# Attention output made by token and transposed by DMA, in batches 4 to 7 of a fused attention and bilinear FFN kernel

## Chip, cores, metric

One core of one Trainium2 chip. The metric is device time in microseconds (us) of one execution; times quoted are medians of several runs. The engines are PE (TensorE matmuls; PEld is its weight loading), VectorE (DVE in the profile), ScalarE (ACT), GpSimd (POOL) and SyncE (SP, which here only issues DMAs). In the timelines below each works through its own instructions in program order; the wait of 12.96 us shown there comes of it. The rounds ran on several chips, and each ratio compares runs of the same rounds. In this text a profile line such as "L255" is line 255 of that kernel; the changed kernel has other numbers for the same code.

## The reference

```python
# q, k, v: (8 batches, 8 heads, 576 tokens, 64), float32
kv  = einsum('bhsd,bhse->bhde', k, v)            # 64x64 per head
o   = einsum('bhsd,bhde->bhse', q, kv)
rms = sqrt(mean(o * o, axis=-1) + 1e-6)          # over the 64 of a head
x   = (o / rms * g_norm)  -> (4608 tokens, 512)
out = ((x @ w_a) * (x @ w_b)) @ w_out            # 512 -> 1536 -> 512
```

## The kernel before

The FFN runs in nine strips of 512 tokens (numbered from 0). A strip is 12 units (4 matmuls with w_a, 4 with w_b; ScalarE copies the first sum, VectorE multiplies the second by it: "ab product"), then 4 output groups of 12 matmuls. The x of batch s+1 is made in the gaps of strip s. It is made with the features on partitions, as the FFN needs it: product, square, a matmul with a block of ones (which sums the squares over a head's 64 partitions and copies the sum to all of them), root, product with g.

```python
    def psq(self, p, i0):                                   # ScalarE
        nc.scalar.activation(sq[p % 3], P[:, i0 : i0 + 2, 0:HF], AF.Square)
    def pss(self, p, i0, hs=(0, 1)):                        # PE, ScalarE
        for h in hs:
            nc.tensor.matmul(P[:, i0 + h, 0:HF], lhsT=ones, rhs=sq[p % 3][:, h, :], ...)
        nc.scalar.activation(rs[p % 3][...], P[...], AF.Abs_reciprocal_sqrt, bias=eps_t)
    def pst(self, p, x0, hs=(0, 1)):                        # VectorE: P * g * rs -> xt[p]
        ...
    def x(self, p, i0):                                     # PE, 288 columns each
        for h in range(2):
            nc.tensor.matmul(P[:, i0 + h, 0:HF], lhsT=kvb[self.b % 2][:, p, :],
                             rhs=self.qT[:, p, h * HF : (h + 1) * HF], ...)

def load_late(b):                                           # all on GpSimd
    if b > EARLY:
        nc.gpsimd.tensor_copy(gate, qT[(b - 1) % 2][0:1, 0, 0:1])   # waits for a q transpose
    ...                       # six DMA issues: q to a DRAM buffer (2), k (2), v (2)

def transpose_q(b):
    nc.sync.dma_start_transpose(qT[b % 2], qs_d[b])

for s in range(1, N_STRIP - 1):
    b = s + 1
    A = Attn(b) if b < B else None
    for n in range(FC + 4):
        amid = (lambda n=n: slot(A, s, n - 0.5)) if A else None
        ...                                   # FFN unit or output group n; amid() inside it
        if A:
            slot(A, s, n)                     # a piece of the work for x of batch b
        if n == 8 and b + 1 < B:
            if s > 1:
                transpose_q(b + 1)
                if b + 2 < B:
                    load_late(b + 2)
            ...
```

The gate is a one-element copy that keeps the late load of batch b+2 from starting before the q of batch b+1 has been transposed. [cuts are marked by "..."]

## Time and profile before

| | before |
|---|---|
| time, median of 4 runs beside the changed kernel | 321.39 us (321.21 to 322.28) |
| span in the profile, granted PE clock | 319.4 us, 1.000 |
| strips 1 to 6, each | 33.9 us |

Lines of the page of the kernel before: busy time by engine, the granted clock in 40 slices (9 is 90% or more), the chain that ended last, and groups of instructions (line, engine, operation, output<-inputs, shapes, count | busy us, mean ns | idle before it and who ended that).

```profile
PE 312.0 (98%) x1848; PEld 150.2 (47%) x1883; DVE 124.6 (39%) x218; ACT 125.3 (39%) x217; POOL 70.2 (22%) x94
...
PEclk9999999999999999999999999999999999999999
...
PE 93%; POOL 3%; DMA 2%; issue 1%; ACT 0%; POOLq 0%
...
L273 DVE TENSOR_TENSOR ab<-P,asb 128x512 bf16<-128x512 f32 x108 | 74.5, 691 | 124.0 <-PE P L255 120.7
...
L126 POOL COPY gate<-qT 1x1 bf16<-1x1 bf16 x5 | 0.9, 176 | 83.2 <-DMA qT<-qs 83.2
L209 PE MATMUL P<-sq,ones 128*128 128x288 bf16 x64 | 13.2, 286 | 0.5 <-ACT sq L205 0.4
L235 PE MATMUL P<-qT,kvb 128*128 128x288 bf16 x56 | 11.4, 286 | 0.0
```

PE is the limit: it is busy nearly all the time and is nearly all of the chain. The mean of 286 ns is the length of one matmul's record; the records overlap, and the timeline shows a pair of these matmuls taking 0.24 us from its first start to the start of what follows, 0.12 us each. VectorE idles 120.7 us waiting for PE (L273), so it has room.

Stretches of the kernel before: start:end, length, then busy us of PE, PEld, DVE, ACT, POOL, granted clock, DMA share, GB/s. These are strips 3 to 5.

```profile
118.33:152.22 33.89, 33.73 (x198) 16.28 (x200) 13.45 (x22) 14.39 (x24) 7.00 (x8) 1.00 1.26 151
152.22:186.12 33.90, 33.69 (x198) 16.29 (x200) 13.45 (x22) 14.39 (x24) 6.57 (x7) 1.00 0.73 102
186.12:220.02 33.90, 33.69 (x198) 16.30 (x200) 13.45 (x22) 14.39 (x24) 0.00 (x0) 1.00 0.17 46
```

Timeline of the kernel before around the late load of strip 4, SyncE's and GpSimd's queues (start, length, engine, line, operation).

```profile
153.39 2.24 SPq L141 DMA_TRANSPOSE qT<-qs  x1
159.02 0.18 POOL L126 COPY gate<-qT 1x1 bf16<-1x1 bf16 x1 [19.17 <-DMA qT<-qs]
159.50 3.26 POOL L129 DMA_DIRECT2D qs<-in_q_dram  x2 [0.30 <-issue]
...
165.18 0.72 POOL L136 DMA_DIRECT2D vtl<-in_v_dram  x1
```

GpSimd stands at the gate for 19.17 us. That costs nothing here, as nothing else is queued on it. Note two lengths: 5.6 us from the issue of the transpose to the gate, and 6.9 us from the gate to the end of the last issue.

### The profile page before, as it was taken

To read this page: it belongs to the slowest core of one execution; us is meant where nothing else is said; L and a number is where in the kernel's file an instruction comes from. 1 tells how busy PE (TensorE), PEld (TensorE's weight loads), DVE (VectorE), ACT (ScalarE), POOL (GpSimd) and SP (SyncE) were. 2 spreads that over 40 slices of the span, in tenths; PEclk is the share of its full clock that TensorE was granted. 3 is DMA by queue.
4 is the path that set the end of the run, shared out by engine and by line. 5 is a ranking of instruction groups with operands and counts; after the bars stand their busy time and mean duration, and the time that the engine had idled before them with its cause. 6 is when DMAs were issued, how large, how long until landed. Compare 5 with 4: busy or idle time off the path is not lost.

```text
span 319.4 us, 4695 instructions
## 1 busy us (share of the span) xinstructions
PE 312.0 (98%) x1848; PEld 150.2 (47%) x1883; DVE 124.6 (39%) x218; ACT 125.3 (39%) x217; POOL 70.2 (22%) x94
## 2 busy tenths in 40 slices
PE   8899999999999999999999999999999999999995
PEld 3444454444445444444444444444544444444443
DVE  5543344444244333452245324532364243313421
ACT  3733165354335443542445225542454323123310
POOL 8944990070043080350070000000000000000000
PEclk9999999999999999999999999999999999999999
DMA  8999999999379999899499150003000200020002
GB/s 182 197 196 199 201 182 230 141 95 161 99 92 159 135 123 211 81 138 173 119 94 129 66 139 2 0 35 100 0 2 14 90 30 0 34 84 18 0 33 99
DMA packets 79308, 32.60 MB, mean 102 GB/s; under 512 B 49974, under 2 KB 74806, under 8 KB 79286
## 3 DMA queue, kind: packets, MB, share of 16 engines
q0 software_dynamic: 59120, 18.44, 53.0%
q1 hardware_dynamic: 19810, 13.44, 17.1%
q10 hardware_dynamic: 356, 0.43, 0.4%
q8 instruction: 14, 0.23, 0.3%
q14 instruction: 8, 0.07, 0.1%
HBM read 37.75 MB, written 12.98 MB: 159 GB/s over the span
## 4 chain that ended last, share of the span: by engine, by line
PE 93%; POOL 3%; DMA 2%; issue 1%; ACT 0%; POOLq 0%
PE P L255 58%; PE P L309 29%; PE P L209 2%; PE P L235 2%; DMA wb_t<-in_moe_w_b_dram 2%; PE P L158 2%; POOL vt L106 1%; POOL qt L106 1%; POOL kt L106 1%; PE P L182 0%; POOL wa_t L367 0%; POOL wb_t L367 0%; ACT o_end L540 0%; POOL ident masks.py:199 0%; POOL ident masks.py:197 0%
## 5 line engine op out<-in xcount | busy, mean ns | idle before, releaser
L273 DVE TENSOR_TENSOR ab<-P,asb 128x512 bf16<-128x512 f32 x108 | 74.5, 691 | 124.0 <-PE P L255 120.7
L255 PE MATMUL P<-xt,wa_t 128*128 128x512 bf16 x422 | 111.2, 379 | 0.9 <-issue 0.2
L255 PE MATMUL P<-xt,wb_t 128*128 128x512 bf16 x421 | 110.1, 379 | 0.3
L309 PE MATMUL P<-wo_t,ab 128*128 128x512 bf16 (+1 forms) x431 | 97.5, 373 | 0.7
L269 ACT CAST asb<-P 128x512 bf16<-128x512 f32 x108 | 63.0, 585 | 85.3 <-PE P L255 83.8
L255 PEld LDWEIGHTS <-wb_t 128*128 128x128 bf16 x432 | 42.3, 98 | 50.6 <-DMA wb_t<-in_moe_w_b_dram 0.5
L309 PEld LDWEIGHTS <-ab 128*128 128x128 bf16 x444 | 43.1, 98 | 45.4
L255 PEld LDWEIGHTS <-wa_t 128*128 128x128 bf16 x432 | 41.7, 98 | 45.1 <-issue 0.5
L223 DVE SCALAR_TENSOR_TENSOR xt<-P,g_col,rs 128x288 bf16<-128x288 f32 x64 | 30.1, 513 | 29.6 <-ACT rs L213 29.6
L205 ACT ACTIVATE sq<-P 128x576 bf16<-128x576 f32 x31 | 20.2, 650 | 25.1 <-PE P L235 23.2
L213 ACT ACTIVATE rs<-P,eps_t 128x576 f32<-128x576 f32 (+1 forms) x33 | 23.9, 727 | 14.9 <-PE P L209 14.6
L322 ACT COPY osb<-P 128x512 f32<-128x512 f32 x17 | 10.0, 586 | 46.0 <-PE P L309 43.6
L324 DVE COPY osb<-P 128x512 f32<-128x512 f32 x18 | 12.4, 691 | 26.9 <-PE P L309 26.8
L129 POOL DMA_DIRECT2D qs<-in_q_dram x12 | 19.6, 1636 | 2.2 <-issue 2.1
L126 POOL COPY gate<-qT 1x1 bf16<-1x1 bf16 x5 | 0.9, 176 | 83.2 <-DMA qT<-qs 83.2
L209 PE MATMUL P<-sq,ones 128*128 128x288 bf16 x64 | 13.2, 286 | 0.5 <-ACT sq L205 0.4
L235 PE MATMUL P<-qT,kvb 128*128 128x288 bf16 x56 | 11.4, 286 | 0.0
L169 ACT CAST kvb<-P 64x256 bf16<-64x256 f32 (+1 forms) x20 | 6.0, 301 | 11.1 <-PE P L158 11.0
L209 PEld LDWEIGHTS <-ones 128*128 128x128 bf16 x64 | 6.2, 98 | 7.5 <-issue 0.4
L235 PEld LDWEIGHTS <-kvb 128*128 128x128 bf16 x56 | 5.5, 98 | 6.0
L121 POOL DMA_DIRECT2D wo_t<-in_moe_w_out_dram x12 | 6.4, 530 | 6.7 <-DMA wb_t<-in_moe_w_b_dram 3.3
L337 PE MATMUL P<-zeros 128*128 128x512 bf16 x16 | 6.2, 532 | 1.2 <-DVE eps_t L352 1.2
(55 smaller groups left out, 82.6 us busy)
## 6 DMA issues: line engine op xcount, KB each, us to landing
out_dram<-osb SPq DMA_DIRECT2D x23, 256.0 KB, 2.0
qs<-in_q_dram POOLq DMA_DIRECT2D x12, 288.0 KB, 6.6
ktl<-in_k_dram POOLq DMA_DIRECT2D x6, 512.0 KB, 8.7
vtl<-in_v_dram POOLq DMA_DIRECT2D x6, 512.0 KB, 10.7
out_dram<-osb SPq DMA_DIRECT2D x13, 128.0 KB, 2.4
wo_t<-in_moe_w_out_dram POOLq DMA_DIRECT2D x12, 128.0 KB, 6.0
wa_t<-in_moe_w_a_dram POOLq DMA_DIRECT2D x5, 256.0 KB, 9.2
wb_t<-in_moe_w_b_dram POOLq DMA_DIRECT2D x5, 256.0 KB, 9.8
```

What stands on the lines that cost most here:

```text
L129: nc.gpsimd.dma_start(out=d[:, hs, :], in_=q[b, hs].rearrange("h t d -> t h d"))
L205: nc.scalar.activation(sq[p % 3], P[:, i0 : i0 + 2, 0:HF], AF.Square)
L209: nc.tensor.matmul(P[:, i0 + h, 0:HF], lhsT=ones, rhs=sq[p % 3][:, h, :], start=True, stop=True)
L213: nc.scalar.activation(rs[p % 3][:, h0:h1, :], P[:, i0 + h0 : i0 + h1, 0:HF], AF.Abs_reciprocal_sqrt, bias=eps_t,)
L223: nc.vector.scalar_tensor_tensor(out=xt[p][:, t0 : t0 + HF], in0=P[:, x0 + h, 0:HF], scalar=g_col, in1=rs[p % 3][:, h, :], op0=ALU.mult, o ...
L235: nc.tensor.matmul(P[:, i0 + h, 0:HF], lhsT=kvb[self.b % 2][:, p, :], rhs=self.qT[:, p, h * HF : (h + 1) * HF], start=True, stop=True,)
L255: nc.tensor.matmul(self.a if w is wa_t else self.b, lhsT=w[:, kc, self.fc * 128 : (self.fc + 1) * 128], rhs=xt[kc][:, t0 : t0 + STRIP], st ...
L269: nc.scalar.copy(self.t, self.a)
L273: nc.vector.tensor_mul(abt[self.s % 2][self.fc], self.b, self.t)
L309: nc.tensor.matmul(P[:, i, e0:e1], lhsT=abt[s % 2][fc][:, g * 128 : (g + 1) * 128], rhs=wo_t[:, fc, e0:e1], start=(fc == 0), stop=(fc == F ...
L322: nc.scalar.copy(t, P[:, i, :])
L324: nc.vector.tensor_copy(t, P[:, i, :])
```

## The change

The intent is to take work off PE. For batches 4 to 7, x is made with tokens on partitions, in five chunks of 128, 128, 128, 128 and 64 tokens. Then the sum of squares of a head is a sum along a row, which VectorE does here (0.67 us a chunk in the changed kernel's trace), and the matmul with ones goes. The result must be turned, which a DMA transpose does from one part of SBUF to another (in that trace it took SyncE 1.2 us to issue and landed in 2.4 us, medians of 20). x becomes one tile, so that one transpose can write all four K chunks; g is loaded onto all partitions (`g_all`). The x products lie in `x_tok`, which shares its memory with a buffer of the opening; in the profile both are called `q_x`.

```diff
-    xt = [sb([128, n_tok], BF16, f"xt{i}") for i in range(KC)]
+    xt = sb([128, KC, n_tok], BF16, "xt")
...
+    def tx(self, c, i):                      # PE: 4 matmuls of 128 columns; ScalarE: square
+        t0 = c * 128
+        n = min(128, S - t0)
+        for p in range(NP):
+            nc.tensor.matmul(P[0:n, i, p * 128 : (p + 1) * 128],
+                             lhsT=self.qT[:, p, t0 : t0 + n], rhs=kvb[self.b % 2][:, p, :], ...)
+        nc.scalar.activation(sqt[c % 2][0:n], P[0:n, i, :]..., AF.Square)
...
+    def tss(self, c):                        # VectorE: sum of squares per head
...
+        nc.vector.reduce_sum(sst[c % 2][0:n], sqt[c % 2][0:n], axis=mybir.AxisListType.X)
+    def trs(self, c):                        # ScalarE: root; GpSimd: root * g
...
+        nc.scalar.activation(rst[c % 2][0:n], sst[c % 2][0:n], AF.Abs_reciprocal_sqrt, ...)
+        nc.gpsimd.tensor_mul(sqt[c % 2][0:n], rst[...]..., g_all[...]...)
+    def txt(self, c, i):                     # VectorE: x product; SyncE: DMA transpose
...                                           # t is one of three parts of x_tok, t0 the first token
+        nc.vector.tensor_mul(t[0:n], P[0:n, i, :]..., sqt[c % 2][0:n])
+        nc.sync.dma_start_transpose(xt[:, :, t0 : t0 + n], t[0:n]...)
...
+    nc.sync.dma_start(out=g_all, in_=g_norm.partition_broadcast(128))
...                                           # in slot(A, s, n), after kv at k0
+        if A.b >= BY_TOKEN:                  # BY_TOKEN = 4
+            for c in range(LC + 1):
+                d = n - (k0 + 1.5) - c
+                i = 4 + c % 3
+                if d == 0:
+                    A.tx(c, i)
+                elif d == 0.5:
+                    A.tss(c)
+                elif d == 1:
+                    A.trs(c)
+                elif d == 1.5:
+                    A.txt(c, i)
+            return
```

With k0 = 2 (its value from strip 3 on) the GpSimd products of the five chunks come at n = 4.5, 5.5, 6.5, 7.5 and 8.5. The late load comes at n = 8.

More of the change, by code (lines that the diff above doesn't have):

```diff
@@ L43 @@
     EARLY = 2
+    BY_TOKEN = 4
     KORD = tuple(range(KC))
@@ L75 @@
     rs = [sb([128, 2, HF], FP32, f"rs{i}") for i in range(3)]
+    sqt = [sb([128, H, D], FP32, f"sqt{i}") for i in range(2)]
+    sst = [sb([128, H], FP32, f"sst{i}") for i in range(2)]
+    rst = [sb([128, H], FP32, f"rst{i}") for i in range(2)]
+    g_all = sb([128, D], FP32, "g_all")
     o_sb = [sb([128, d_model], FP32, f"osb{i}") for i in range(4)]
@@ L85 @@
     v32 = sb([EP, 2, EC, D], FP32, "v32")
-    q32 = sb([EP, 2, EC, D], FP32, "q32")
+    q_x = sb([128, 2 * EC * D], FP32, "q_x")
+    q32 = q_x[0:EP].rearrange("p (h c d) -> p h c d", h=2, c=EC)
+    x_tok = q_x.bitcast(BF16).rearrange("p (c h d) -> p c h d", c=3, h=H)
     qc = sb([EP, EC, 2 * D], BF16, "qc")
@@ L223, in pst @@
                 nc.vector.scalar_tensor_tensor(
-                    out=xt[p][:, t0 : t0 + HF],
+                    out=xt[:, p, t0 : t0 + HF],
                     in0=P[:, x0 + h, 0:HF],
@@ L241, in x @@
                 )
+        def tx(self, c, i):
+            t0 = c * 128
+            n = min(128, S - t0)
+            for p in range(NP):
+                nc.tensor.matmul(
+                    P[0:n, i, p * 128 : (p + 1) * 128],
+                    lhsT=self.qT[:, p, t0 : t0 + n],
+                    rhs=kvb[self.b % 2][:, p, :],
+                    start=True,
+                    stop=True,
+                )
+            nc.scalar.activation(
+                sqt[c % 2][0:n], P[0:n, i, :].rearrange("t (h d) -> t h d", h=H), AF.Square
+            )
+        def tss(self, c):
+            n = min(128, S - c * 128)
+            nc.vector.reduce_sum(sst[c % 2][0:n], sqt[c % 2][0:n], axis=mybir.AxisListType.X)
+        def trs(self, c):
+            n = min(128, S - c * 128)
+            nc.scalar.activation(
+                rst[c % 2][0:n],
+                sst[c % 2][0:n],
+                AF.Abs_reciprocal_sqrt,
+                bias=eps_t[0:n],
+                scale=1.0 / D,
+            )
+            nc.gpsimd.tensor_mul(
+                sqt[c % 2][0:n],
+                rst[c % 2][0:n].unsqueeze(2).to_broadcast([n, H, D]),
+                g_all[0:n].unsqueeze(1).to_broadcast([n, H, D]),
+            )
+        def txt(self, c, i):
+            t0 = c * 128
+            n = min(128, S - t0)
+            t = x_tok[:, c % 3]
+            nc.vector.tensor_mul(
+                t[0:n], P[0:n, i, :].rearrange("t (h d) -> t h d", h=H), sqt[c % 2][0:n]
+            )
+            t0 += self.b * S
+            nc.sync.dma_start_transpose(
+                xt[:, :, t0 : t0 + n], t[0:n].rearrange("t h d -> t (h d)")
+            )
     class Unit:
@@ L257, in mm @@
                     lhsT=w[:, kc, self.fc * 128 : (self.fc + 1) * 128],
-                    rhs=xt[kc][:, t0 : t0 + STRIP],
+                    rhs=xt[:, kc, t0 : t0 + STRIP],
                     start=(kc == KORD[0]),
```

## The prediction

> **What bounds the kernel.** TensorE. The page's first part has PE busy 98%; in the chain that ended last PE is 93%; granted clock is 1.00. A table by stretches shows strip 4 (152.2 to 186.1 us): PE busy 33.7 of 33.9 us, VectorE 13.5, ScalarE 14.4, GpSimd 6.6 (only DMA issue). Work given to others is free unless PE waits for it.
>
> **Removed and added on PE.** In the timeline a pair of 288-column matmuls takes 0.24 us. Batches 4 to 7 lose 32 product and 32 square-sum matmuls: 64 x 0.12 = 7.7 us. They gain 80 matmuls of 128 columns; scaled from 0.216 us per 512 columns, an estimated 0.054 us each, 4.3 us. Gain: 3.4 us (1%).
>
> **Added elsewhere.** Per chunk of 128 tokens: ScalarE a square (0.6 us, like the 128x512 cast, 585 ns) and a tiny root; VectorE a sum[...] and a product out of PSUM (0.69, like the ab product); GpSimd a 128x512 product[...].
>
> **Two new waits.**
> 1. The instruction order on VectorE is ab product, x product(c), sum(c+1). A chunk is a ring: sum, root, GpSimd product, x product[...], while PE wants a unit (8 matmuls plus 4 new ones) every 1.95 us. In-order VectorE then delays ab products[...].
> 2. The large one. In strips 3 and 4 the fifth chunk's GpSimd product is queued behind the late load: four products, gate copy, six DMA issues, fifth product. The gate waits for the next batch's q transpose, which SyncE now issues only after the x transposes of chunks 0 to 3. Before, in strip 4, that transpose was issued at 153.4 and the gate ran at 159.0 us, harmlessly early; gate to last issue took 6.9 us. After: [...]q transpose 5.6, gate and issues 6.9, [...]x product and next ab product 1.5: about 16 us from chunk 3's x product, of which PE covers 4 to 5 (two units, half an output group). Chunk 4's x product blocks VectorE, hence ab 10 and 11, hence PE: an estimated 12 us of PE idle in each of strips 3 and 4. Strips 5 and 6 have no late load.
> Such idling should drop PE's clock[...]. Before shows slow matmuls only at its opening (532 against 379 ns).
>
> **Sum.** 321.5 - 3.4 + 24[...] = 349.5 us: predicted 349 us, range 335 to 361. Faster by over 2%: 0.03; within 2%: 0.09; slower by over 2%: 0.88.
>
> **What will show it.** PE idle of 8 to 15 us in strips 3 and 4, released by VectorE's ab product; VectorE's x product waiting for GpSimd; gates at two thirds of those strips instead of the first quarter to half; strips 5 and 6 within 2.5 us of 33.9; 128-column matmuls 0.055 to 0.06 us apart[...].
>
> **What would make it wrong.** A q transpose landing far from 5.6 us;[...] weight loads of 128-column matmuls not hidden.

Passages that rest on figures which no run of this case had shown are cut. The sum came to 349.5 us; two of its terms are cut, one for a lower clock after the large waits and one for the ring on VectorE, so what stands of it does not add up to that. Two of the pieces behind the "about 16 us" are cut as well. Those that stand come to 14.0 us, which would leave 9 to 10 us of PE idle a strip instead of 12. The trace of the changed kernel gives what the cut passages were about: 0.67 us for a sum on VectorE, 1.04 us for a 128x512 product on GpSimd (1.09 for the fifth), 1.2 us to issue an x transpose, 2.77 us a turn of the ring, and a granted clock of 0.86 and 0.89 in strips 3 and 4.

## The result, and the profile after

| | before | after |
|---|---|---|
| time, median of 4 runs | 321.39 us (321.21 to 322.28) | 356.27 us (353.21 to 357.85) |
| ratio | | 1.107 (95% interval 1.098 to 1.115) |
| span in the profile, granted clock | 319.4 us, 1.000 | 355.7 us, 0.952 |
| first output matmul starts at | 35.4 us | 40.0 us |
| strips 1 and 2 | 33.9, 33.9 us | 33.9, 33.9 us |
| strips 3 and 4 | 33.9, 33.9 us | 48.5, 48.3 us |
| strips 5 and 6 | 33.9, 33.9 us | 35.2, 35.2 us |

A ratio is the mean time of one kernel's fast runs over that of the other's of the same rounds, so it is not quite the ratio of the medians. A strip is measured from its first FFN matmul to the next strip's.

Lines of the page of the changed kernel that answer to those above.

```profile
PE 319.4 (90%) x1864; PEld 150.4 (42%) x1899; DVE 133.1 (37%) x226; ACT 117.3 (33%) x225; POOL 91.4 (26%) x114
...
PEclk9599999999999999956999959999999999999999
...
PE 78%; POOL 6%; DMA 5%; issue 5%; DVE 4%; ACT 1%; DVEq 0%; SPq 0%; POOLq 0%
...
L366 PE MATMUL P<-wo_t,ab 128*128 128x512 bf16 (+1 forms) x431 | 101.4, 387 | 22.0 <-DVE ab L330 21.4
L312 PE MATMUL P<-xt,wa_t 128*128 128x512 bf16 x422 | 111.1, 379 | 7.0 <-DVE ab L330 6.2
...
L282 POOL TENSOR_TENSOR sqt<-rst,g_all 128x512 f32<-128x512 f32 (+1 forms) x20 | 20.9, 1047 | 106.4 <-ACT rst L275 106.4
...
L292 DVE TENSOR_TENSOR q_x<-P,sqt 128x512 bf16<-128x512 f32 (+1 forms) x20 | 13.8, 690 | 39.4 <-POOL sqt L282 39.3
...
L271 DVE TENSOR_REDUCE sst<-sqt 128x8 f32<-128x512 f32 (+1 forms) x20 | 13.5, 674 | 0.0
```

PE now waits 27.6 us for ab products of VectorE, and VectorE waits 39.3 us in its x products (L292) for GpSimd. VectorE's busy time grew from 124.6 to 133.1 us, which is 37% of the longer span: it looks held rather than overloaded, and experiment 4 tests that. The clock dips in three places: it is 0.54 from 10 to 20 us, 0.86 in strip 3 and 0.89 in strip 4.

The same stretches of the changed kernel: its opening, then strips 3, 4 and 5.

```profile
10.00:20.00 10.00, 8.92 (x88) 4.27 (x89) 4.01 (x10) 4.99 (x9) 9.14 (x13) 0.54 1.40 197
122.98:171.45 48.47, 36.28 (x202) 16.36 (x204) 15.53 (x24) 12.36 (x26) 12.50 (x13) 0.86 0.88 117
171.45:219.71 48.26, 35.77 (x202) 16.27 (x204) 15.52 (x24) 12.36 (x26) 11.87 (x12) 0.89 0.59 84
219.71:254.87 35.16, 33.39 (x202) 15.79 (x204) 15.53 (x24) 12.36 (x26) 5.21 (x5) 1.00 0.25 61
```

The timeline of the changed kernel in strip 3, PE, VectorE, GpSimd and SyncE's queue around the late load.

```profile
142.82 1.04 POOL L282 TENSOR_TENSOR sqt<-rst,g_all 128x512 f32<-128x512 f32 x1 [1.73 <-ACT rst L275]
...
143.89 0.69 DVE L292 TENSOR_TENSOR q_x<-P,sqt 128x512 bf16<-128x512 f32 x1 [0.89 <-POOL sqt L282]
...
145.98 2.24 SPq L151 DMA_TRANSPOSE qT<-qs  x1
...
147.55 2.32 PE L366 MATMUL P<-wo_t,ab 128*128 128x512 bf16 x10
150.67 0.18 POOL L136 COPY gate<-qT 1x1 bf16<-1x1 bf16 x1 [6.81 <-DMA qT<-qs]
...
156.90 0.72 POOL L146 DMA_DIRECT2D vtl<-in_v_dram  x1
157.60 1.09 POOL L282 TENSOR_TENSOR sqt<-rst,g_all 64x512 f32<-64x512 f32 x1
158.72 0.68 DVE L292 TENSOR_TENSOR q_x<-P,sqt 64x512 bf16<-64x512 f32 x1 [12.96 <-POOL sqt L282]
159.33 1.27 DVE L330 TENSOR_TENSOR ab<-P,asb 128x512 bf16<-128x512 f32 x2
159.44 1.17 SPq L296 DMA_TRANSPOSE xt<-q_x  x1
160.06 0.61 PE L366 MATMUL P<-wo_t,ab 128*128 128x512 bf16 x1 [10.20 <-DVE ab L330]
```

Read it from the bottom. PE stands for 10.20 us until VectorE has made an ab product. VectorE had PE's data long before (the last matmuls of these units ended at 147.71 us, the ab product began at 159.33), but the x product of the fifth chunk stood ahead of it in VectorE's queue, and that waited 12.96 us for GpSimd. GpSimd had the fifth product behind the late load: it waited for the q transpose until 150.67 and then issued six DMAs until 157.6. The q transpose was issued only at 145.98, behind the x transposes of four chunks. Three engines' queues pass one wait on to PE.

The theory from here on: (1) the queue of the late load on GpSimd makes the two long waits of strips 3 and 4; (2) the order of VectorE's instructions makes the short waits of all four strips; (3) the opening, which I had not foreseen, is slowed by the load of g. Rivals: the DMA transposes or their traffic hold PE up; VectorE has too much work; the opening is chance.

### The profile page after: what moved, and what is told of

Same layout as the page of the kernel before. It is cut to its first block, busy times and chain, and to the rows that moved or that the text cites. A ratio compares the mean times of both kernels' runs of the same rounds, so it can differ in the third digit from the quotient of the medians.

```text
span 355.7 us, 4848 instructions
## 1 busy us (share of the span) xinstructions
PE 319.4 (90%) x1864; PEld 150.4 (42%) x1899; DVE 133.1 (37%) x226; ACT 117.3 (33%) x225; POOL 91.4 (26%) x114
## 4 chain that ended last, share of the span: by engine, by line
PE 78%; POOL 6%; DMA 5%; issue 5%; DVE 4%; ACT 1%; DVEq 0%; SPq 0%; POOLq 0%
PE P L312 44%; PE P L366 26%; POOL sqt L282 3%; DMA qT<-qs 3%; DVE sst L271 2%; DMA qt<-in_q_dram 2%; PE P L168 2%; PE P L219 1%; DVE ab L330 1%; PE P L192 1%; PE P L245 1%; PE P L258 1%; POOL qs L139 1%; ACT rst L275 1%; PE P L206 1%
## 5 line engine op out<-in xcount | busy, mean ns | idle before, releaser
L366 PE MATMUL P<-wo_t,ab 128*128 128x512 bf16 (+1 forms) x431 | 101.4, 387 | 22.0 <-DVE ab L330 21.4
L282 POOL TENSOR_TENSOR sqt<-rst,g_all 128x512 f32<-128x512 f32 (+1 forms) x20 | 20.9, 1047 | 106.4 <-ACT rst L275 106.4
L381 DVE COPY osb<-P 128x512 f32<-128x512 f32 x18 | 12.5, 692 | 48.4 <-PE P L366 38.9
L292 DVE TENSOR_TENSOR q_x<-P,sqt 128x512 bf16<-128x512 f32 (+1 forms) x20 | 13.8, 690 | 39.4 <-POOL sqt L282 39.3
L233 DVE SCALAR_TENSOR_TENSOR xt<-P,g_col,rs 128x288 bf16<-128x288 f32 x32 | 15.1, 512 | 14.5 <-ACT rs L223 14.5
L223 ACT ACTIVATE rs<-P,eps_t 128x576 f32<-128x576 f32 (+1 forms) x17 | 12.0, 713 | 10.1 <-PE P L219 10.1
L215 ACT ACTIVATE sq<-P 128x576 bf16<-128x576 f32 x15 | 9.8, 650 | 13.2 <-PE P L245 8.5
L271 DVE TENSOR_REDUCE sst<-sqt 128x8 f32<-128x512 f32 (+1 forms) x20 | 13.5, 674 | 0.0
L275 ACT ACTIVATE rst<-sst,eps_t 128x8 f32<-128x8 f32 (+1 forms) x20 | 6.0, 301 | 21.2 <-DVE sst L271 21.2
L265 ACT ACTIVATE sqt<-P 128x512 f32<-128x512 f32 (+1 forms) x20 | 11.6, 582 | 0.0
L258 PEld LDWEIGHTS <-qT 128*128 128x128 bf16 (+1 forms) x80 | 5.9, 100 | 5.5 <-issue 1.7
```

Source lines behind the costliest of these rows:

```text
L223: nc.scalar.activation(rs[p % 3][:, h0:h1, :], P[:, i0 + h0 : i0 + h1, 0:HF], AF.Abs_reciprocal_sqrt, bias=eps_t,)
L233: nc.vector.scalar_tensor_tensor(out=xt[:, p, t0 : t0 + HF], in0=P[:, x0 + h, 0:HF], scalar=g_col, in1=rs[p % 3][:, h, :], op0=ALU.mult, o ...
L265: nc.scalar.activation(sqt[c % 2][0:n], P[0:n, i, :].rearrange("t (h d) -> t h d", h=H), AF.Square)
L271: nc.vector.reduce_sum(sst[c % 2][0:n], sqt[c % 2][0:n], axis=mybir.AxisListType.X)
L282: nc.gpsimd.tensor_mul(sqt[c % 2][0:n], rst[c % 2][0:n].unsqueeze(2).to_broadcast([n, H, D]), g_all[0:n].unsqueeze(1).to_broadcast([n, H, D]),
L292: nc.vector.tensor_mul(t[0:n], P[0:n, i, :].rearrange("t (h d) -> t h d", h=H), sqt[c % 2][0:n])
```

## The experiments

All kernels gave correct results. Each edit is against the changed kernel unless said otherwise.

### 1. The late load after the fifth product

```diff
                     transpose_q(b + 1)
-                    if b + 2 < B:
+                    if b + 2 < B and b < BY_TOKEN:
                         load_late(b + 2)
...
+            if n == 10 and b >= BY_TOKEN and b + 2 < B:
+                load_late(b + 2)
```

> The late load of strips 3 and 4 (gate copy and six DMA issues on GpSimd) is issued two units later, after the fifth chunk's GpSimd product; everything else as in the changed kernel. Theory 1 (the fifth product is stuck behind the late load in GpSimd's order): the PE waits of 10.2 and 10.4 us vanish, the clock stays 1.00 there, and strips 3 and 4 become like strips 5 and 6 (35.2 us instead of 48.5 and 48.3); the time falls by 26 to 27 us, to about 329 us (328 to 332). Rival (the DMA transposes, their number on SyncE or their traffic, hold PE up): they are all still there at the same places, so the time stays within 5 us of 356.

Measured: 328.26 us (327.72 to 331.4), ratio 1.023 to the kernel before. Strips 3 and 4 are 35.1 us, like 5 and 6. These are its stretches for strips 3 and 4; the clock is 1.00 again.

```profile
119.57:154.66 35.09, 33.60 (x205) 15.79 (x204) 15.52 (x24) 12.36 (x26) 12.36 (x14) 1.00 0.82 113
154.66:189.81 35.15, 33.60 (x205) 15.78 (x204) 15.52 (x24) 12.36 (x26) 12.13 (x13) 1.00 0.82 119
```

The same GpSimd work is in these strips, and the same transposes. Only the order on GpSimd changed, and 26.5 us went in these two strips. (The time fell by 28 us; the opening happened to be shorter in some of these runs, for which see experiments 5 and 6.) The rival of the transposes falls.

### 2. The fifth product on VectorE, the late load left in place

```diff
+            eng = nc.vector if c == LC else nc.gpsimd
-            nc.gpsimd.tensor_mul(
+            eng.tensor_mul(
```

> Only the small product root times g of the fifth chunk moves from GpSimd to VectorE; the late load, the gate and the transposes keep their places and the gate still waits late. Theory 1: no engine that PE needs is behind the gate any more, so strips 3 and 4 fall to about 35 us, total about 329 us (327 to 332), with the gate copy still running at two thirds of these strips. Rival (late transposes or late loads in themselves cost the time): strips 3 and 4 stay near 48 us, total 350 or more.

Measured: 333.16 us (332.18 to 335.38), ratio 1.035. The mechanism is as expected and the size is missed. The gate of strip 3 still runs late, and yet the strip has the length of strip 5, where there is no late load. Its timeline on GpSimd, and its stretches for strips 3 and 5:

```profile
150.99 0.18 POOL L136 COPY gate<-qT 1x1 bf16<-1x1 bf16 x1 [6.74 <-DMA qT<-qs]
```

```profile
123.20:159.35 36.15, 33.60 (x206) 15.76 (x204) 16.22 (x25) 12.36 (x26) 11.35 (x12) 1.00 0.84 112
195.48:231.62 36.14, 33.60 (x206) 15.73 (x204) 16.21 (x25) 12.36 (x26) 4.16 (x4) 1.00 0.60 101
```

So a late gate and a late load cost nothing in themselves; only an instruction that PE needs behind them does. The extra 1 us in each of four strips (36.1 against 35.2) is the price of the edit: the product (0.68 us), and before it a wait of 0.37 us for its root, now stand ahead of an ab product in VectorE's own queue, and the longest PE wait of a strip grew from 0.9 to 1.9 us.

### 3. The q transpose early

```diff
+        if BY_TOKEN <= b and b + 1 < B:
+            transpose_q(b + 1)
         for n in range(FC + 4):
...
-                    transpose_q(b + 1)
+                    if b < BY_TOKEN:
+                        transpose_q(b + 1)
```

> In strips 3 to 6 the q transpose is issued at the start of the strip, ahead of the x transposes; the late load keeps its place in GpSimd's order, ahead of the fifth product. Theory 1 splits the wait in two: the gate's wait (6.8 and 7.3 us in the trace) goes, the issues (6.9 us) stay, so PE still waits about 3.5 to 4 us in strips 3 and 4, the clock falls less or not at all, and the total is 338 to 345 us. If the q transpose's late landing were all of it, the total would be 329 us; if it had no part, 356 us.

Measured: 339.42 us (336.69 to 340.78), ratio 1.055, inside the range. GpSimd's timeline in strip 3 shows a gate that no longer waits, and the issues that remain:

```profile
139.83 1.04 POOL L282 TENSOR_TENSOR sqt<-rst,g_all 128x512 f32<-128x512 f32 x1 [1.73 <-ACT rst L275]
140.81 0.18 POOL L136 COPY gate<-qT 1x1 bf16<-1x1 bf16 x1
...
147.38 1.09 POOL L282 TENSOR_TENSOR sqt<-rst,g_all 64x512 f32<-64x512 f32 x1
```

PE's longest wait is 3.0 us in strips 3 and 4 (10.2 and 10.4 before the edit). The wait of 10 us was thus some 7 us of gate and 3 us of issues. Without a late load (strip 5 of the changed kernel) the fifth product starts 2.83 us after the fourth. Here it started 4.7 us later than that, and in the changed kernel 11.95 us later; so in both PE's stock of work covered about 1.7 us of the delay.

Strip 3 is 38.6 us and strip 4 40.4, although their waits are equal: in strip 4 the clock fell after the pause, in strip 3 it did not (granted 0.96 and 1.00). The record of the granted clock shows where these two differ. In the trace of the changed kernel the clock was 0.50 in stretches of 10.24, 13.65 and 10.24 us (and in the last 0.56 us), and the six times at which the three begin and end lie on one grid of 3.41 us. In the trace of this experiment a stretch of half clock lasts 3.41 us. These are the stretches between grid points around the two pauses:

```profile
145.35:148.77 3.42, 1.52 (x8) 0.49 (x5) 0.27 (x1) 0.00 (x0) 3.12 (x4) 1.00 2.13 153
148.77:152.18 3.41, 2.13 (x10) 0.90 (x11) 2.30 (x4) 0.00 (x0) 0.00 (x0) 1.00 1.56 188
186.31:189.73 3.42, 1.03 (x4) 0.40 (x5) 2.09 (x4) 0.00 (x0) 0.81 (x1) 1.00 1.50 163
189.73:193.14 3.41, 3.41 (x9) 1.21 (x8) 0.48 (x1) 0.00 (x0) 0.00 (x0) 0.50 1.51 184
```

Strip 3's pause was split between two stretches, with 1.52 and 2.13 us of PE work in them, and the clock stayed. Strip 4's pause fell mostly into one, with 1.03 us of PE work, and in the next the clock was half. No limit follows from this: in the opening of the changed kernel the clock fell after a stretch with 2.0 us of PE work (5.60 to 9.01 us), in which PE had paused for 1.2 us.

### 4. The ring cut on VectorE

```diff
-            for c in range(LC + 1):
+            for c in range(LC + 1) if n % 1 else reversed(range(LC + 1)):
```

At whole n this puts the sum of chunk c+1 ahead of the x product of chunk c.

> VectorE takes the sum of chunk c+1 before the x product of chunk c, so the ring sum, root, GpSimd product, x product (2.77 us a turn in the trace, against 1.95 us of PE work) is cut; the late load stays where it is. Theory: strips 5 and 6 lose their PE waits (1.6 us) and fall from 35.2 to 33.1 us, 0.8 below the kernel before; strips 3 and 4 keep waits of 10 us or somewhat more. Total 350 to 356 us, near 352. Rival (VectorE's added work of 1.37 us a chunk, not the order, is too much for it): strips 5 and 6 stay at 34.5 us or more.

Measured: 345.62 us (344.87 to 349.54), ratio 1.078. This is below the range that I had written: strips 3 and 4 gained too (45.7 and 46.8 against 48.5 and 48.3 us). Strip 5 of this kernel:

```profile
215.35:248.63 33.28, 33.28 (x205) 15.80 (x204) 15.72 (x24) 12.93 (x26) 5.20 (x5) 1.00 0.27 64
```

No PE wait is left in strips 5 and 6, and they are 0.6 us shorter than before the change. VectorE is busy 15.7 of 33.3 us there, more than in the ring version: it was its order that cost time, not its load.

### 5 and 6. The load of g

Experiment 5 moves the load of g to the first output stage. Experiment 6 adds the load, at its early place and unused, to the kernel before.

```diff
 # 5, against the changed kernel
-    nc.sync.dma_start(out=g_all, in_=g_norm.partition_broadcast(128))
...
     nc.sync.dma_start(out=gate_d, in_=vt[1][0:1, H - 1, EC - 1, D - 1 : D])
+    nc.sync.dma_start(out=g_all, in_=g_norm.partition_broadcast(128))
 # 6, against the kernel before
+    g_all = sb([128, D], FP32, "g_all")
...
+    nc.sync.dma_start(out=g_all, in_=g_norm.partition_broadcast(128))
```

> Only the load of g onto 128 partitions moves, from the first microseconds to about the first output stage. The changed kernel's opening is 4.7 us longer than before's in the profile (first output matmul at 40.2 instead of 35.5 us, clock down in it, PE waiting 1.2 us for the first q tile). Theory: the broadcast load, issued at 1.7 us, delays the first q load, PE pauses and its clock falls; then the opening is 35.5 us again and the total falls by 3 to 5 us, to about 352. Rival (the other changes to the opening, the single x tile or chance): the opening stays at about 40 us and the total at 356.

> The kernel before, with nothing added but that load of g onto 128 partitions at the same place in the program (its result unused). Theory: the opening grows by up to 4.7 us as in the changed kernel, total 323 to 327 us with more scatter between runs than before's 1 us. Rival: no effect, 321.4 us.

Measured: experiment 5 351.57 us (351.28 to 351.98, clock 0.971 in all four runs), ratio 1.093; its first output matmul starts at 35.6 us. Experiment 6 325.70 us (322.37 to 326.24), ratio 1.010 (1.007 to 1.014); its first output matmul starts at 38.9 us in the profile. The longest wait of PE in experiment 6 (us in total, times, longest), and its stretch from 10 to 20 us:

```profile
PE P L183 <- DMA qt<-in_q_dram: 1.3, 1, 1.3
```

```profile
10.00:20.00 10.00, 9.80 (x94) 4.50 (x95) 4.58 (x12) 5.88 (x11) 9.06 (x13) 0.68 1.40 196
```

The load of 32 KB (128 copies of 256 bytes) is issued 0.2 us after the first q load of GpSimd and takes 6.3 us to land. The three q loads of these microseconds then land in 7.4 us (median) instead of 5.3, PE pauses for 1.3 us, and the clock falls to 0.68 of full speed from 10 to 20 us (before: 1.00). The scatter of the runs comes from the same place: with the load late it is 0.7 us, with it early 3.9 us, and 4.6 us in the changed kernel. Both directions agree, so the load of g is the cause and not chance. Whether the clock falls does vary: in the profiled run of experiment 1, with the same early load, PE paused for 0.6 us, the clock stayed at 1.00 and strip 3 began at 119.57 us (changed kernel 122.98, before 118.33).

### 7. All three repairs

The edits of experiments 1, 4 and 5 together.

> The changed kernel with the late load after the fifth product, the sum before the x product, and the load of g later. If the three causes are all there is, what stays is the saving on PE of 3.4 us (64 matmuls of 288 columns against 80 of 128): 318 us, a ratio of 0.989 to the kernel before; strips 3 to 6 at about 33.1 us each. If a part is missing, 320 to 325 us.

Measured: 319.33 us (319.17 to 319.65), ratio 0.993 (0.992 to 0.994). Faster than both kernels, though by only 0.7% than the one before, but 1.3 us above what I expected: strips 3 to 6 take 33.28 us, a gain of 0.62 each and not 0.85. No wait of PE is left in them; this is strip 3:

```profile
118.43:151.71 33.28, 33.28 (x205) 15.77 (x204) 15.72 (x24) 12.91 (x26) 11.85 (x12) 1.00 0.86 121
```

Starts of matmuls in the trace give the rest. Four full chunks cost 0.22 us each (0.055 a matmul, as estimated). The chunk of 64 tokens costs about 0.43: its first matmul starts 0.31 us after the one before it instead of 0.22, and the first matmul after it 0.15 us later instead of 0.06.

### 8. The fifth chunk with 128 tokens

The last chunk takes the last 128 tokens of the batch, so 64 tokens are made twice, with equal values. The edit is against experiment 7.

```diff
-            t0 = c * 128
-            n = min(128, S - t0)
+            t0 = min(c * 128, S - 128)
+            n = 128
...                                           # n = 128 likewise in tss, trs and txt, t0 in txt
```

> As the kernel with all three repairs, but the fifth chunk takes the last 128 tokens of the batch (64 of them a second time) instead of 64. In that kernel's trace the four matmuls of the 64-token chunk cost PE 0.43 us instead of 0.22: their 64-column weight load starts 0.31 us after the matmul ahead of it began (0.22 for full loads), and the way back costs 0.15 instead of 0.06. Theory: the half-wide weight load is what keeps strips 3 to 6 at 33.28 instead of 33.05 us; they become 33.07 us each and the time falls by 0.85 us, from 319.3 to about 318.5. Rival (the cost is in the batch's last chunk whatever its width): 319.3.

Measured: 318.22 us (318.01 to 318.37), ratio 0.989 (0.9875 to 0.991). Strips 3 to 6 are 33.05 us. So twice the tokens in the chunk are faster: the width of 64 was the cost. By what means was not shown: the runs do not tell it from a cost of switching between widths.

### 9. Batch 3 as well

The edit is against experiment 8.

```diff
-    BY_TOKEN = 4
+    BY_TOKEN = 3
...
-            if n == 10 and b >= BY_TOKEN and b + 2 < B:
+            if n == (10 if s > 2 else 13) and b >= BY_TOKEN and b + 2 < B:
```

> The same, with batch 3 made by token as well (its late load issued after its fifth product). If PE's work is all that counts, strip 2 falls from 33.9 to about 33.1 us as well, total about 317.7 us, ratio 0.988 to the kernel before. If VectorE's added work in strip 2 or a late x in strip 3 makes PE wait, 318.5 us or more.

Measured: 317.15 us (316.99 to 317.29), ratio 0.986 (0.984 to 0.988); strip 2 is 33.05 us too. This is the best version run. The last strip gave another 0.3 us, for which I have no cause.

## Why the prediction was right, and where it was not

Predicted were 349 us, with a range of 335 to 361, and slower by over 2% at 0.88. Measured were 356.27 us. The table sets the terms of the predicted sum beside what the trace of the changed kernel shows.

| term | predicted, us | shown, us |
|---|---|---|
| PE work saved | -3.4 | -2.5 (4 x 0.62, strips of experiment 7) |
| PE idle behind the late load | +24 | +21.4 (output matmuls waiting for ab products) |
| half clock after it | (cut) | about +4.5 (20 matmul starts 0.427 instead of 0.216 us apart, and two between) |
| ring on VectorE, four strips | (cut) | about +7.5 (strip 5: 35.16 less 33.28 us is 1.9) |
| opening | 0 | +4.7 (first output matmul 40.0 against 35.4 us) |
| sum, with the cut terms | +28 | about +36 (spans: 36.3) |

- The large wait was right in place, length and cause: predicted 12 us a strip, shown 10.2 and 10.4 at a stretch, in strips 3 and 4 only. The pieces of the chain that stand were right as well: q transpose 5.6 (4.7 from issue to gate), gate and issues 6.9 (6.9). For the two that are cut the trace shows 1.2 us (issue of an x transpose) and 1.09 us (GpSimd's fifth product). The gates ran at 57% and 58% of these strips, where two thirds were forecast. Experiments 1 to 3 show that the order on GpSimd is the cause, and divide it.
- The ring was right in kind (2.77 us a turn shown, against the 1.95 us of PE work a unit), but its term, an estimate, was too small: it was 1.9 us a strip, 7.5 us in all. Experiment 4 shows it.
- The clock term: a fall was foreseen and is shown (0.86 and 0.89 in strips 3 and 4). The trace shows 6.0 and 5.0 us at half clock from the first matmul to full speed, with a pause of 0.4 us in it: PE resumed inside a stretch of the 3.41 us grid of experiment 3, and full speed came at the end of the next one (162.6 to 166.0 and 210.4 to 213.8 us), the first that PE filled (3.41 us of work in each).
- The saving on PE was too high by 0.9 us in all: "scaled from 0.216 us per 512 columns" held for the full chunks and failed for the half-wide one (experiment 8).
- What the prediction left out is the opening. It treated the small load of g as nothing, and did not ask what it is ahead of or beside. It is the largest missing term, 4.7 us, and experiments 5 and 6 show it.

So the direction and the main cause were understood, but that the number fell inside the range owes something to the width of the range (26 us): the sum came out about 7 us short, and 4.7 us of that is a term that I had left out.

Not settled: why the last strip is 0.2 us longer in the changed kernel (34.77 against 34.55 us); and what makes the clock fall: half clock followed stretches of the 3.41 us grid with 1.03 and 2.0 us of PE work, and did not follow those with 1.52 and 2.13 us.

## What to carry to other kernels

Before an instruction goes to an idle engine, list what that engine's queue holds ahead of it, and what that waits for: here GpSimd's wait at the gate (6.8 us) and its issues (6.9 us) became a PE wait of 10.2 us. A chain over several engines that came back to VectorE, which takes its instructions in order, set VectorE's pace by its latency (2.77 us a turn against 1.95 us of PE work, 1.9 us a strip); start step one of the next item before the last step of this one, as experiment 4 did. A small load in a tight opening was not free (32 KB, 4.7 us later at the first output matmul): place it when its data are needed.
